# An H3 convolution and MLP stack: first block, first loads and first change of units rewritten

## The chip, the cores and the metric

The kernel runs on one core of a Trainium2 chip. A core has five engines with a queue each, worked in order: PE (TensorE, matmuls), DVE (VectorE), ACT (ScalarE), POOL (GpSimd) and SP (SyncE, which issues here all DMAs). The metric is the device time of one execution in microseconds; several executions are timed and their median is given. The profile of one execution gives the span of the program's instructions on the engines, and its own time.

## The reference

The input x is 2048 tokens by 1024 channels, fp32. Two layers follow each other twice, with the same weights both times:

```python
x = A_q
x = x + _A_ref(_layernorm(x, axis=-1), A_k, A_v, A_shift_k, A_ssm_k, A_ssm_D)
x = x + _B_ref(_layernorm(x, axis=-1), B_w1, B_b1, B_w2, B_b2)
x = x + _A_ref(_layernorm(x, axis=-1), A_k, A_v, A_shift_k, A_ssm_k, A_ssm_D)
x = x + _B_ref(_layernorm(x, axis=-1), B_w1, B_b1, B_w2, B_b2)
```

`_A_ref(q, k, v, ...)` shifts k by a four-tap causal filter, multiplies with v, convolves the product over the 2048 tokens with a long filter of each channel (through FFTs), adds `kv * ssm_D`, and multiplies with q. The convolution does not depend on x, so its result y serves both A layers; only the gate `layernorm(x) * y` is done twice. `_B_ref` is `relu(x @ w1 + b1)**2 @ w2 + b2` with 3584 hidden units.

## The kernel before

**Tiling.** Tokens are cut into 4 blocks of 512, and a block into 4 tiles of 128 tokens. A *unit* is one MLP layer on one block; ORDER gives the order of the units as (layer, block): (0,0), (1,0), (0,1), (0,2), (1,1), (0,3), (1,2), and the last entry does two blocks together. A unit runs over four chunks of 7 slices of 128 hidden units: steps of kind m1 (x times a piece of w1) and m2 (hidden times a piece of w2). A step is 12 or more matmuls of one weight piece of 128x512.

**Split numbers.** A matmul on fp32 is done as three on rounded numbers: each operand is a high part (a cast by ACT) and a low part (operand minus high part, a subtraction by DVE or POOL), lines 356, 357, 358. A weight piece is loaded by SP into `wr`, cast by ACT (line 1112) into the first half of `whl`, and its low part is made by DVE or POOL (line 1120; the letters in WLO choose). Some pieces are stored split (`wd_m`) and later loaded again as they are. `xh`, `xl` are the high and low part of the transposed, normalized input of a unit.

**The convolution** runs beside the MLP. A forward stream (`fwd_x`, `fwd_g`) brings k, v and the filter into another base: DMAs, ACT, DVE (lines 386 to 388 make the shifted product `fx`), PE transposes of it (line 441), PE matmuls (412, 475), DVE sums (504, 505), stores. A product stream multiplies (POOL, line 546, tile `cp`) and sums (DVE, line 550), goes back by PE (line 616), and stores y. After each MLP step the program runs some of each stream: `pace` gives how many products per step, FWD_RATE the forward steps. So the place of line 441's transposes in PE's queue is fixed when the program is written; PE waits there if DVE has not made `fx` yet.

**The first block** (`first_block`) does the convolution for block 0 without a stream: in a `Plan`, tasks with costs, dependencies and buffer rings are listed, and a search of 400 tries orders them by a list schedule. In it, for each of 8 groups c of 128 channels, x_part (lines 1227 to 1251) and g_part (1286 to 1293) are transforms on PE (line 1194) with a copy by ACT after each, `prods_both` multiplies them (1389 to 1403, DVE or POOL), `behind` goes back by PE, gates with the normalized q (1459) and adds to q (1468). `ln_part` takes the layernorm of q: bn_stats on DVE (1324), bn_aggr (1330), the reciprocal root by ACT Sqrt and six small DVE operations (1335 to 1344), and the scaling (1355 on DVE, 1358 on ACT). At its end the same is done for the gated sum (`tail_stats`, `tail_moments`, `tail`), with transposes (1498) and the splits into `xh`, `xl` (1505, 1507); the first weight pieces (`weight`, 1517, 1518) are loaded there too, and their matmuls are the first of unit 0. Filters need a patch: row 0 of the filter tile of a group is overwritten by a 1x128 DMA from the tile `first` (filter plus ssm_D). In the trace this is `xh<-xh`; `xh<-kT` is k, `fx<-vT` is v, `xh<-ssmT` the filter, `yh<-fwd` and `xh<-pro` the transform tables (all these live in the memory of `xh`, `yh`).

**The first change of units** goes from unit (0,0) to (1,0), on the same tokens, so the output of the last chunk is gated and normalized on the spot, for tiles 0 and 1 and then for 2 and 3 (`chain`), while PE does half steps of the other tiles (steps with fewer than 4 tiles). `evict1` adds the result to `accs` and takes bn_stats (1768, 1769), stage 0 and 1 make the scale (1735, 730 to 747, 1744), stage 2 gates (ACT 1750, DVE 1757, 1759) and takes bn_stats again (1763), stages 3 and 4 make the second scale, 5 and 6 normalize (1798, 1800), 7 and 8 transpose (1809), 9 and 10 split (1817, 1818). CHAIN gives for each stage after how many steps it is written.

Of the kernel before, what the change touches and what calls it, by code (L numbers as in the profile page):

```python
# [20 lines left out]
P = 128  # L21
# [31 lines left out]
PAD_C, PAD_P, PAD_M = 104, 56, 32  # L53
# [13 lines left out]
CHAIN = ((2, 3, 3, 7, 8, 8, 9, 13, 13, 14, 14), (2, 3, 3, 7, 8, 8, 9, 12, 12, 13, 13))  # L67
NORM = "VAVA"
# [181 lines left out]
def tile_h3_mlp(ctx: ExitStack, tc: tile.TileContext, q, kT, vT, shk, ssmT, ssmD, w1, b1, w2, b2,  # L250
# [54 lines left out]
    SY.dma_start(sgn, sgn_t)  # L305
    eph = const.tile([P, 2], F32)
    V.memset(eph[:, 0:1], EPS)
    V.memset(eph[:, 1:2], -0.5)
# [9 lines left out]
    SY.dma_start(b1t[:, 0:FT], b1)  # L318
# [838 lines left out]
    def first_block():  # L1157
# [24 lines left out]
        def dma(dst, src, r=(), w=(), cost=740, key=None):  # L1182
            pl.add([("D", cost)], lambda e: SY.dma_start(dst(), src()), r, w, lat=2000)

        with tc.tile_pool(name="pro", bufs=1) as pro:
# [19 lines left out]
            def kv_load(c):  # L1205
                k4 = sub("k4", 3, 0, [P, T + 3])
                v4 = new(cv, "fx", 4, [P, T])
                dma(lambda: k4.t, lambda: kT[c * P:(c + 1) * P, 0:T + 3], w=[k4])
                dma(lambda: v4.t, lambda: vT[c * P:(c + 1) * P, 0:T], w=[v4])
                return k4, v4  # L1210
# [13 lines left out]
            def x_part(c, k4, v4):  # L1224
# [14 lines left out]
                for r in range(2):  # L1239
# [7 lines left out]
                    pl.add([("PE", 1850)], mm, [xt, *tabs], [oi])  # L1247
# [10 lines left out]
            def g_load(c):  # L1258
                raw = sub("lg", 2, 1560, [P, T])
                for e in range(2):  # L1260
                    dma(lambda e=e: raw.t[:, e * BL:e * BL + BL].rearrange("p (b c) -> p b c", b=BT),
                        lambda e=e: g_rows(0, c)[:, e], w=[(raw, e)], cost=370)
                dma(lambda: raw.t[0:1, 0:P], lambda: first.t[c:c + 1, 0:P], [first], [(raw, 0)], cost=10)
# [63 lines left out]
            def moments(st, n):  # L1327
# [5 lines left out]
                ve, sd, r, nm = (new(pre, nm, m, [P, n]) for nm, m in (("ve", 3), ("sd", 3), ("rs", 4), ("nm", 3)))  # L1333
                t = new(pre, "rt", 2, [P, n])
                pl.add([("V", 140, 1)], lambda e: V.tensor_scalar(ve.t, mv.t[:, :, 1], EPS, None, op0=OP.add),
                       al, [ve], lat=130)
                pl.add([("A", 190)], lambda e: A.activation(sd.t, mv.t[:, :, 1], AF.Sqrt, bias=epst), al, [sd])
                pl.add([("V", 140, 1)], lambda e: V.reciprocal(r.t, sd.t), [sd], [r], lat=130)
                pl.add([("V", 140, 1)], lambda e: V.tensor_mul(t.t, r.t, r.t), [r], [t], lat=130)
                pl.add([("V", 140, 1)], lambda e: V.tensor_mul(t.t, t.t, ve.t), [ve], [t], lat=130)  # L1340
# [386 lines left out]
    def chain(accs, b, xh, xl, ready):  # L1727
# [4 lines left out]
        def agg(st):  # L1732
            mv = st["mv"] = pre.tile([P, 2, 2], F32, name="mv3", bufs=2)
            for n in range(2):
                V.bn_aggr(mv[:, n], st["st"][:, n])
# [629 lines left out]
```

## Time and profile before

| what | value |
|---|---|
| median of 3 runs | 2678.97 us (2678.12 to 2685.03) |
| the profiled execution | 2684.3 us |
| its span | 2682.5 us |
| PE busy | 2623.8 us (98%) |
| DVE busy | 1985.1 us (74%) |
| ACT busy | 1124.1 us (42%) |
| POOL busy | 1034.1 us (39%) |
| DMA moved | 763.16 MB, 284 GB/s over the span |
| mean granted TensorE clock | 0.994 |

A page lists the busy time of each engine, the chain of work that ended last, and the groups of instructions with their mean duration and the idle time before them. Here one engine is busy nearly all the time, so what is left to win or lose stands in its idle stretches, and in the stretches in which its clock was granted at half rate. They are found with the view of waits (who waited for whom), with the timeline (idle time before an instruction in brackets, with its releaser), and with windows (busy time and granted clock of a stretch).

### The profile page before, as it was taken

To read this page: it belongs to the slowest core of one execution; us is meant where nothing else is said; L and a number is where in the kernel's file an instruction comes from. 1 tells how busy PE (TensorE), PEld (TensorE's weight loads), DVE (VectorE), ACT (ScalarE), POOL (GpSimd) and SP (SyncE) were. 2 spreads that over 40 slices of the span, in tenths; PEclk is the share of its full clock that TensorE was granted. 3 is DMA by queue.
4 is the path that set the end of the run, shared out by engine and by line. 5 is a ranking of instruction groups with operands and counts; after the bars stand their busy time and mean duration, and the time that the engine had idled before them with its cause. 6 is when DMAs were issued, how large, how long until landed. Compare 5 with 4: busy or idle time off the path is not lost.

```text
span 2682.5 us, 36122 instructions
## 1 busy us (share of the span) xinstructions
PE 2623.8 (98%) x12388; PEld 2199.4 (82%) x12388; DVE 1985.1 (74%) x2881; ACT 1124.1 (42%) x1915; POOL 1034.1 (39%) x675
## 2 busy tenths in 40 slices
PE   7999899899999999999999999999999999999999
PEld 6888787787888888888888888888788778888887
DVE  7979788788887878779767775456778668777553
ACT  3444244343435323343233422345444585454342
POOL 2436665155551744417454275100100217536111
PEclk9999999999999999999999999999999999999999
DMA  7789988689989998888987888689889797878653
GB/s 247 255 306 310 296 291 283 240 282 357 348 296 315 313 331 307 275 292 308 337 307 261 297 292 314 201 273 312 299 298 307 263 340 255 263 249 316 232 193 121
DMA packets 380265, 763.16 MB, mean 284 GB/s; under 512 B 44064, under 2 KB 159408, under 8 KB 377008
## 3 DMA queue, kind: packets, MB, share of 16 engines
q1 hardware_dynamic: 380080, 760.85, 83.0%
q8 instruction: 98, 1.61, 0.2%
q14 instruction: 87, 0.71, 0.1%
HBM read 583.49 MB, written 177.21 MB: 284 GB/s over the span
## 4 chain that ended last, share of the span: by engine, by line
PE 79%; DMA 8%; DVE 5%; POOL 2%; issue 2%; ACT 2%; SPq 1%; DVEq 0%; POOLq 0%; ACTq 0%
PE p L357 23%; PE p L356 23%; PE p L358 23%; DMA whl<-wd_m 2%; PE pt L358 2%; PE pt L357 2%; PE pt L356 2%; PE p L1194 2%; DMA wr<-w 2%; DMA cg<-gd 1%; DVE whl L1120 1%; POOL cp L546 1%; DMA wd_m<-whl 0%; PE p L817 0%; DVE sm L550 0%
## 5 line engine op out<-in xcount | busy, mean ns | idle before, releaser
L546 POOL TENSOR_TENSOR cp<-cx,cg 128x384 f32<-128x384 f32 (+5 forms) x288 | 542.0, 1895 | 574.7 <-DVE sm L550 362.2
L356 PE MATMUL p<-xh,whl 128*128 128x512 f32 (+1 forms) x1504 | 578.4, 385 | 5.6 <-DMA whl<-wd_m 5.6
L358 PE MATMUL p<-xh,whl 128*128 128x512 f32 (+1 forms) x1504 | 574.1, 382 | 3.3 <-DVE whl L1120 2.8
L357 PE MATMUL p<-xl,whl 128*128 128x512 f32 (+1 forms) x1504 | 574.1, 382 | 0.1
L1112 ACT CAST whl<-wr 128x512 fp32r<-128x512 f32 x546 | 332.5, 619 | 468.4 <-PE p L358 278.6
L1120 DVE TENSOR_TENSOR whl<-wr,whl 128x512 fp32r<-128x512 f32 x486 | 421.0, 877 | 135.0 <-ACT whl L1112 130.2
L356 PE MATMUL p<-whl,rh 128*128 128x512 f32 x1204 | 475.4, 395 | 6.0 <-DMA whl<-wd_m 5.2
L357 PE MATMUL p<-whl,rh 128*128 128x512 f32 x1204 | 471.2, 391 | 2.8 <-POOL whl L1120 1.7
L358 PE MATMUL p<-whl,rl 128*128 128x512 f32 x1204 | 470.6, 391 | 0.0
L356 PEld LDWEIGHTS p<-xh,whl 128*128 128x128 f32 x1504 | 284.7, 189 | 60.8 <-issue 4.9
L358 PEld LDWEIGHTS p<-xh,whl 128*128 128x128 f32 x1504 | 284.2, 189 | 58.2 <-DVE whl L1120 3.0
L357 PEld LDWEIGHTS p<-xl,whl 128*128 128x128 f32 x1504 | 284.5, 189 | 52.4 <-DVE xl L1507 0.3
L1597 DVE TENSOR_TENSOR rl<-wr,rh 128x512 fp32r<-128x512 f32 x140 | 138.6, 990 | 182.5 <-ACT rh L1594 182.4
L1120 POOL TENSOR_TENSOR whl<-wr,whl 128x512 fp32r<-128x512 f32 x60 | 86.7, 1448 | 484.4 <-ACT whl L1112 438.1
L356 PEld LDWEIGHTS p<-whl,rh 128*128 128x128 f32 x1204 | 227.3, 189 | 54.1 <-issue 3.3
L357 PEld LDWEIGHTS p<-whl,rh 128*128 128x128 f32 x1204 | 227.1, 189 | 50.2 <-DVE whl L1120 2.7
L358 PEld LDWEIGHTS p<-whl,rl 128*128 128x128 f32 x1204 | 227.0, 189 | 47.5
L550 DVE TENSOR_REDUCE sm<-cp 128x128 f32<-128x384 f32 (+5 forms) x288 | 249.4, 874 | 12.3 <-POOL cp L546 12.3
L1589 ACT ACTIVATE wr<-p,b1t 128x512 f32<-128x512 f32 x138 | 95.2, 690 | 371.9 <-PE p L358 371.0
L1717 DVE TENSOR_TENSOR acc<-p,acc 128x512 f32<-128x512 f32 x152 | 99.7, 686 | 81.3 <-PE p L358 81.3
L696 POOL TENSOR_TENSOR sm<-sm 128x512 f32<-128x512 f32 x48 | 69.1, 1440 | 132.4 <-DVE sm L550 118.8
L358 PE MATMUL p<-whl,tq 128*128 128x512 f32 x276 | 107.4, 389 | 0.0
(384 smaller groups left out, 4282.3 us busy)
## 6 DMA issues: line engine op xcount, KB each, us to landing
whl<-wd_m SPq DMA_DIRECT2D x318, 512.0 KB, 5.6
wr<-w SPq DMA_DIRECT2D x442, 256.0 KB, 5.6
wd_m<-whl SPq DMA_DIRECT2D x70, 512.0 KB, 6.1
wr<-td SPq DMA_DIRECT2D x112, 256.0 KB, 5.1
cx<-xd SPq DMA_DIRECT2D x48, 512.0 KB, 5.7
cg<-gd SPq DMA_DIRECT2D x48, 512.0 KB, 7.0
tq<-hd SPq DMA_DIRECT2D x24, 1024.0 KB, 6.9
gd<-fg SPq DMA_DIRECT2D x72, 256.0 KB, 6.7
```

The source lines that it names most:

```text
L356: PE.matmul(o, lh, rh, start=start, stop=False)
L357: PE.matmul(o, lh, rl, start=False, stop=False)
L358: PE.matmul(o, ll, rh, start=False, stop=stop)
L546: G.tensor_mul(pr.rearrange("p c i -> p i c"), xt[:, 0:j + 1], gt[:, j::-1])
L550: V.tensor_reduce(sm[:, ty, jj], st["pr"], axis=AX.X, op=OP.add)
L696: E.tensor_add(s[:, 1:3], s[:, 1:3], s[:, 0:1].to_broadcast([P, 2, s.shape[2]]))
L1112: A.copy(t[:, 0], raws[n]["t"])
L1120: ENG[e[n % len(e)]].tensor_sub(t[:, 1], raws[n]["t"], t[:, 0].bitcast(F32))
L1194: PE.matmul(o, lh, r, start=start, stop=stop)
L1589: A.activation(r, st["o"], AF.Relu, bias=b1t[:, st["f"]:st["f"] + 1])
L1597: V.tensor_sub(st["lo"], st["r"]["t"], st["hi"].bitcast(F32))
L1717: V.tensor_add(accs[tt][:, d], o, accs[tt][:, d])
```

## The change

1. **Statistics of the first block on ACT.** `ln_part` no longer uses bn_stats: for each of the four tiles of q one ACT pass (Copy with scale -1/1024 and accum_out) sums the tile to minus its mean, and one (Square with that as bias) sums the squared differences. The reciprocal root is one `pow` with -0.5 on POOL, with two or three small POOL operations around it, here and in `moments`, which the tail keeps using after bn_stats. Scaling on DVE now is multiply and add with r and -mean*r.
2. **Ordered first loads, later weights.** HEAD ranks the first DMAs: k, the row for the patch, v, the filter, the tables. `sgn` and `b1` are loaded after them. The loads of the first eight weight pieces depend on a matmul of group 4 (W_AFTER, the key "late").
3. **The first change of units.** Tile 0 (or 2) of a half gets its sum from `scalar_tensor_tensor` with accum_out in the add itself (`summed`, 1742 after), and its squares from one ACT pass (`spread_a`, 1748 after); the other tile keeps bn_stats. Scales are made one tile at a time by three POOL operations (`scale_of`, 1758 to 1760 after). Gating is staged: tile 0 in stage 1, tile 1 in stage 2, with the normalization of tile 0 between them. CHAIN's numbers change, the splits of tile 2 and 3 come one or two steps earlier, NORM is "AAVA".
4. **Pace.** In half steps no products are run (rate 0 instead of a tenth), and PACE_SLACK for blocks 1 and 2 goes from 74 to 80, which spreads the same products over fewer steps. Weights are advanced before the streams in all half steps. PAD_P, a spacer in memory, goes from 56 to 120 columns.

Core of the diff:

```diff
@@
-PACE_SLACK = {1: 74, 3: 10}
+HEAD = {"k": 0, "f": 1, "v": 2, "g": 3, "t": 4, "p": 5, "d": 6}
+W_AFTER = 4
+PACE_SLACK = {1: 80, 3: 10}
-CHAIN = ((2, 3, 3, 7, 8, 8, 9, 13, 13, 14, 14), (2, 3, 3, 7, 8, 8, 9, 12, 12, 13, 13))
-NORM = "VAVA"
+CHAIN = ((2, 3, 5, 7, 8, 6, 9, 13, 13, 14, 14), (2, 3, 5, 7, 8, 6, 9, 11, 12, 12, 13))
+NORM = "AAVA"
@@ first_block
+            rank = 0 if head is None else HEAD[head] * 1e7 - 1e9
+            pl.add([("D", cost)], lambda e: SY.dma_start(dst(), src()), r, w, lat=2000, rank=rank)
@@ moments, ln_part
-                pl.add([("A", 190)], lambda e: A.activation(sd.t, mv.t[:, :, 1], AF.Sqrt, bias=epst), al, [sd])
-                pl.add([("V", 140, 1)], lambda e: V.reciprocal(r.t, sd.t), [sd], [r], lat=130)
...
+                pl.add([("G", 900)], lambda e: G.tensor_tensor(r.t, ve.t, eph[:, 1:1 + n], op=OP.pow), [ve], [r], lat=130)
+                pl.add([("G", 250)], lambda e: G.tensor_mul(nm.t, nm.t, r.t), [r], [nm], lat=130)
...
-                    for i in range(2):
-                        half_stats(st, k, x, i, keys[4 * i:4 * i + 4])
-                moments(st, len(ts))
+                    pl.add([("A", 1130)], lambda e, x=x, t=t, k=k: A.activation(
+                        ns[t].t, x.t, AF.Copy, scale=-1.0 / D, accum_out=nm.t[:, k:k + 1]), keys, [(nm, k), *spare])
+                    pl.add([("A", 1230)], lambda e, x=x, t=t, k=k: A.activation(
+                        ns[t].t, x.t, AF.Square, bias=nm.t[:, k:k + 1], accum_out=ss.t[:, k:k + 1]),
+                        [(nm, k), *keys], [(ss, k), *spare])
@@ chain
+        def summed(st, n, d, z):
+            x = accs[st["tts"][n]][:, d * 512:(d + 1) * 512]
+            V.scalar_tensor_tensor(x, z, 1.0, x, op0=OP.mult, op1=OP.add, accum_out=st["c"][:, 4 + d:5 + d])
+        def spread_a(st):
+            c = st["c"]
+            V.tensor_scalar(c[:, 0:1], c[:, 4:5], c[:, 5:6], -1.0 / (root * D), op0=OP.add, op1=OP.mult)
+            junk = ml.tile([P, D], BF16, name="yt", bufs=2)
+            A.activation(junk, accs[st["tts"][0]], AF.Square, scale=1.0 / root, bias=c[:, 0:1], accum_out=c[:, 1:2])
+            scale_of(st, 0, c[:, 1:2], c[:, 0:1], root)
+        def scale_of(st, n, var, m, k):
+            o = st["rn"][:, n]
+            G.tensor_add(var, var, epst)
+            G.tensor_tensor(o[:, 0:1], var, eph[:, 1:2], op=OP.pow)
+            G.tensor_scalar(o[:, 1:2], m, o[:, 0:1], k, op0=OP.mult, op1=OP.mult)
...
@@ the steps
-            rate *= 0.1
+            rate = 0.0
```

**What moves on SP, at the start.** Ahead of the change, SP's first loads in the first block:

```order
L1183 DMA xh<-ssmT 8x128
L1183 DMA xh<-kT 128x515
L1183 DMA xh<-ssmD 8x128
L1183 DMA xh<-pro 128x1024
L1183 DMA xh<-ssmT 128x2x128
L1183 DMA fx<-vT 128x512
L1183 DMA yh<-inv 128x256
L1183 DMA xh<-kT 128x515
L1183 DMA xh<-ssmT 128x2x128
L1183 DMA xh<-xh 1x16x8
L1183 DMA yh<-fwd 128x512
```

and with it:

```order
L1184 DMA xh<-kT 128x515
L1184 DMA xh<-ssmT 8x128
L1184 DMA xh<-ssmD 8x128
L1184 DMA fx<-vT 128x512
L1184 DMA xh<-ssmT 128x2x128 x2
L1184 DMA yh<-fwd 128x512
L1184 DMA xh<-pro 128x1024
L1184 DMA xh<-xh 1x16x8
```

The table `fwd` moved from behind the patch to ahead of it, k and v moved forward, and the second k and the table `inv` moved behind the patch.

**What moves on ACT, in the first block.** ACT's queue with the change, from the first copy of a g_part on (L1371 and L1373 are the passes for the statistics, L1238 the copy that x_part's matmuls read, L1357 the scaling):

```order
L1249 COPY sx<-p_218 128x2x4x64
L1373 ACTIVATE cp,sd<-cg,nm 128x1024
L1371 ACTIVATE cp,nm<-cg 128x1024
L1238 COPY fg<-p_261 128x512
L1371 ACTIVATE px,nm<-cx 128x1024
L1373 ACTIVATE cp,sd<-cg,nm 128x1024
L1289 ACTIVATE sg<-p_269 128x2x4x64
L1373 ACTIVATE px,sd<-cx,nm 128x1024
L1228 ACTIVATE p_309<-xh,shkt 128x512
L1373 ACTIVATE cp,sd<-cx,nm 128x1024
L1249 COPY sx<-p_291 128x2x4x64
```

The passes stand between the copies that PE's next matmuls read; before, only the copies and six casts of weights stood there.

**What moves on DVE, in the change of units.** The gating of tiles 2 and 3, ahead of the change (L1757 and L1759 gate, L1763 is bn_stats, L1120 the low part of a weight piece):

```order
L1757 TENSOR_TENSOR p_4978<-p_4978,px 128x512
L1757 TENSOR_TENSOR p_4980<-p_4980,px 128x512
L1759 TENSOR_TENSOR acc<-acc,p_4978 128x512
L1759 TENSOR_TENSOR acc<-acc,p_4980 128x512
L1763 BN_STATS st_4977<-acc 128x6 x2
L1757 TENSOR_TENSOR p_4986<-p_4986,px 128x512
L1757 TENSOR_TENSOR p_4988<-p_4988,px 128x512
L1759 TENSOR_TENSOR acc<-acc,p_4986 128x512
L1759 TENSOR_TENSOR acc<-acc,p_4988 128x512
L1763 BN_STATS st_4977<-acc 128x6 x2
L1120 TENSOR_TENSOR whl<-wr,whl 128x512
```

and with it (L1779 and L1742 gate tile 2, L1779 and L1782 tile 3, L1822 is bn_stats):

```order
L1779 TENSOR_TENSOR p_4878<-p_4878,px 128x512
L1779 TENSOR_TENSOR p_4880<-p_4880,px 128x512
L1742 SCALAR_TENSOR_TENSOR acc,nr<-p_4878,acc 128x512
L1742 SCALAR_TENSOR_TENSOR acc,nr<-p_4880,acc 128x512
L1746 TENSOR_SCALAR nr<-nr 128x1
L1120 TENSOR_TENSOR whl<-wr,whl 128x512
L1779 TENSOR_TENSOR p_4927<-p_4927,px 128x512
L1779 TENSOR_TENSOR p_4929<-p_4929,px 128x512
L1782 TENSOR_TENSOR acc<-acc,p_4927 128x512
L1782 TENSOR_TENSOR acc<-acc,p_4929 128x512
L1822 BN_STATS st_4882<-acc 128x6 x2
```

The weight's low part moved from behind twelve operations of both tiles to behind five of one.

More of the change, by code (lines that the diff above doesn't have):

```diff
@@ L304, in tile_h3_mlp @@
     sgn = const.tile([P, 2], F32)
-    SY.dma_start(sgn, sgn_t)
-    eph = const.tile([P, 2], F32)
+    eph = const.tile([P, NT + 1], F32)
     V.memset(eph[:, 0:1], EPS)
-    V.memset(eph[:, 1:2], -0.5)
+    V.memset(eph[:, 1:], -0.5)
     epst = eph[:, 0:1]
@@ L1515, in weight @@
                 hi, lo = (hl, 0), (hl, 1)
[L1516 removed]
+                dma(lambda: raw.t, lambda: w1[c * FC + f, :, 4 * kh:4 * kh + 4], r=["late"], w=[raw])
                 pl.add([("A", a_cost(512))], lambda e: A.copy(hl.t[:, 0], raw.t), [raw], [hi])
```

161 lines of the change are left out of this document (81 added, 80 removed).

## The prediction

> **What bounds the kernel now.** I read the page first, then the windows by stage, then the waits of PE, then the timeline around each wait.
>
> ```profile
> span 2682.5 us, 36122 instructions
> PE 2623.8 (98%) x12388; PEld 2199.4 (82%) x12388; DVE 1985.1 (74%) x2881; ACT 1124.1 (42%) x1915; POOL 1034.1 (39%) x675
> ```
>
> PE is idle for 2682.5 - 2623.8 = 58.7 us. No matmul leaves the program, so a change of this kind can only win idle time and time at a low clock.
>
> ```profile
> core 0: us, PE busy (x) PEld busy (x) DVE busy (x) ACT busy (x) POOL busy (x), PEclk, DMA share, GB/s
> 0.00:12.50 12.50, 1.10 (x4) 0.74 (x5) 3.48 (x10) 3.19 (x5) 0.69 (x6) 1.00 0.59 176
> 12.50:38.00 25.50, 25.44 (x132) 22.54 (x132) 18.46 (x30) 9.09 (x17) 2.65 (x2) 1.00 0.91 291
> 38.00:60.00 22.00, 18.16 (x98) 16.40 (x99) 20.45 (x29) 10.78 (x20) 8.22 (x7) 0.84 0.75 241
> 60.00:106.00 46.00, 45.79 (x280) 41.93 (x278) 44.09 (x60) 17.12 (x31) 28.01 (x22) 1.00 0.72 224
> 106.00:127.50 21.50, 16.82 (x138) 15.41 (x138) 19.25 (x52) 10.31 (x21) 5.75 (x7) 1.00 0.82 294
> 255.00:310.00 55.00, 45.88 (x206) 38.25 (x206) 47.70 (x68) 19.89 (x37) 32.23 (x27) 0.91 0.90 295
> 475.00:535.00 60.00, 52.09 (x306) 44.79 (x305) 45.07 (x97) 22.56 (x38) 12.77 (x11) 0.97 0.64 230
> 640.00:1900.00 1260.00, 1259.12 (x5882) 1054.08 (x5881) 924.71 (x1313) 470.73 (x826) 506.62 (x278) 1.00 0.86 301
> ```
>
> The idle time is in the start (11.4), the first block (up to 127.5, where unit 0's matmuls begin), unit 0 (255 to 310) and the first change of units (475 to 535). From 640 to 1900 PE is never idle for long: there is nothing to win there. In the first block DVE is nearly as full as PE (44.1 of 46 us), ACT is not.
>
> ```profile
> PE p L441 <- DVE fx L1233: 14.2, 3, 10.4
> PE p L356 <- DMA whl<-wd_m: 10.8, 9, 2.9
> PE pt L441 <- DVE fx L388: 9.8, 4, 7.3
> PE p L358 <- DVE whl L1120: 2.8, 1, 2.8
> PE pt L616 <- DVE fg L505: 2.4, 1, 2.4
> ```
>
> Those are the sums by releaser: DVE ends most of them. A stall has a second cost, the clock after it:
>
> ```profile
> 41.60:47.50 5.90, 5.82 (x21) 0.54 1.02 327
> 304.10:310.20 6.10, 6.05 (x18) 0.53 1.06 294
> 449.00:452.50 3.50, 3.41 (x14) 0.62 0.00 0
> 521.20:525.30 4.10, 4.02 (x21) 0.58 0.56 195
> ```
>
> These windows (PE alone; fourth figure the granted clock) follow the stalls of 3.68, 7.26, 2.35 and 2.79 us. Lost work is (1 - clock) x length: 2.7, 2.9, 1.3 and 1.7 us.
>
> **The start.** PE's first product waits for the table `fwd`, which SP issues behind the patch, which waits for the filter:
>
> ```profile
> 3.68 0.42 SPq L1183 DMA_DIRECT2D xh<-ssmT  x1
> 8.84 0.63 SPq L1183 DMA_DIRECT2D xh<-xh  x1
> 9.51 0.57 SPq L1183 DMA_DIRECT2D yh<-fwd  x1
> 9.52 0.69 DVE L1233 TENSOR_TENSOR fx<-p,fx 128x512 f32<-128x512 f32 x1 [1.03 <-DMA fx<-vT]
> 12.52 2.90 PE L1194 MATMUL p<-fg,yh 128*128 128x256 f32 x6 [1.07 <-DMA yh<-fwd]
> ```
>
> With the change k is issued second and v fifth, and `fwd` no longer waits. But PE's first product is now g_part, which needs the patch. The filter is issued sooner (about 3.2 instead of 3.7) with less ahead of it; by the 5.1 us it took here I put its landing at 7.3 and the patch's issue end at 7.9. The patch of this trace was issued at 8.84 to 9.47 and PE did not ask for it before 17.9; tiny loads issued at that time land in about 2.6 (it is 12.52 - 9.51 = 3.0 for the table). So PE starts at about 10.5: **-2.0** (bounds 0, if the filter lands as late as here, and -3.5).
>
> **The middle of the first block.**
>
> ```profile
> L1324 DVE BATCH_NORM_STATS2 st<-cg 128x6 f32<-128x512 f32 x4 | 2.6, 675 | 0.9 <-DMA cg<-q 0.9
> L1324 DVE BATCH_NORM_STATS2 st<-cx 128x6 f32<-128x512 f32 x4 | 2.5, 672 | 0.0
> 41.68 1.12 PE L441 MATMUL p<-ident,fx 128*128 128x128 f32 x4 [3.68 <-DVE fx L1233]
> L723 ACT ACTIVATE jk<-px,co x8: 1147/1150/1152, 2142.1 to 2191.5; 128x1024 bf16<-128x1024 f32 x8
> L723 ACT ACTIVATION_READ_ACCUMULATOR jk<-px,co x8: 185/186/188, 2143.2 to 2192.5; 128x1 f32 x8
> L725 POOL TENSOR_TENSOR co<-co,eph x8: 550/562/903, 2143.7 to 2193.4; 128x1 f32<-128x1 f32 x8
> ```
>
> DVE loses eight bn_stats, 2.6 + 2.5 = 5.1 us, just ahead of the operations whose lateness stops PE for 3.68 us at 41.68. ACT gains eight passes; line 723 is the same pass late in the program, 1.15 + 0.19, so 8 x 1.34 = 10.7 us. ACT is busy 9.1 of the 25.5 us from 12.5 to 38, so 19.8 fit, but its queue is in order, and the passes stand between the copies that PE reads (L1238 stands behind a pass on the tile of q that is loaded last). Walking the new queues with these durations I find two places where PE waits for ACT, about 1.0 and 1.3 us, and none as long as 3.68. I take 2.3 us of new stalls without a loss of clock: 2.3 - (3.68 + 2.7) = **-4.1**. Bounds: -6.4 (ACT hidden) and 0 (ACT takes over DVE's stall). The later weight loads free POOL and DMA early and cost nothing while their eight casts fit before the first weight matmul; ACT is busy 17.1 of 46 us there.
>
> **The end of the first block.** It is a chain over DVE, ACT and POOL, with PE waiting:
>
> ```profile
> 104.93 0.59 ACT L1248 COPY sx<-p 128x512 f32<-128x512 f32 x1 [1.14 <-PE p L1194]
> 109.69 0.69 DVE L696 TENSOR_TENSOR sm<-sm 128x512 f32<-128x512 f32 x1
> 118.68 0.27 DVE L1330 BATCH_NORM_AGGREGATE mv<-st 128x2 f32<-128x12 f32 x2
> 121.83 0.16 DVE L1344 SCALAR_TENSOR_TENSOR nm<-mv,rs 128x2 f32<-128x2 f32 x1
> ```
>
> The last transform on PE now comes after both pairs of return products instead of ahead of one (+0.9). From its copy to L696 there are 4.8 us here, with eight other DVE operations between; in the new order four, so about 3.3 (-1.4). From bn_aggr to the finished scale there are 3.0 us, six small DVE operations interleaved with four large ones; now four POOL operations, the pow at 0.56, the others shorter: about 1.9 (-1.1). Together **-1.6**, bounds +1 and -4.
>
> **Unit 0.** Nothing in its arithmetic changes, but its order does. The products start later (none in half steps) and are denser by 6 steps in some 230. So the transposes of line 441 come two to four steps later in PE's queue, at another distance from the evictions that fill DVE.
>
> ```profile
> 304.15 1.10 PE L441 MATMUL pt<-ident,fx 128*128 128x128 f32 x4 [7.26 <-DVE fx L388]
> ```
>
> The stalls here sum to 9.8 (L388) + 2.4 (L505), and 2.9 + 1.3 of clock, 16.4 us. The longest came when an eviction and the three shift operations stood close together on DVE; in the new order the next eviction is further ahead of them, and fewer products are done by the end of the unit. But DMA is at 0.90 there, and the backlog started with late loads, which stays. I take **-5**; bounds -16 (all gone) and +10 (one more like the longest, 7.26 + 2.9).
>
> **The change of units.**
>
> ```profile
> 521.28 0.43 PE L358 MATMUL p<-xh,whl 128*128 128x256 f32 x1 [2.79 <-DVE whl L1120]
> ```
>
> In 475 to 535 PE is idle 7.9 us. The longest, 2.79 + 1.7 of clock, waits for a low part that stands behind twelve gating operations on DVE; now it stands behind five, the bn_stats of one tile are gone (0.68 each by the rows above), and the small operations of the root are on POOL. I take 0.7 us for what is left: -3.8. Against it, POOL makes other low parts in this stage, and stands in order behind scales that wait for a 1.34 us pass on ACT; I take -1 for the other 5.1 us. **-4.8**, bounds -9 and +4.
>
> By the Trainium skill's "TensorE: Matmul & The Clock Gate", Part 1: The HAM clock gate, the clock halves after at least one idle window of about 3.4 us; here it halved after 2.35 and 2.79 too. By the page this term would be -3.1.
>
> The stalls on `whl<-wd_m` (10.8 us) lie mostly after the change of units, in an order that is nearly the same: 0, bounds ±4.
>
> **Sum**: -2.0 - 4.1 - 1.6 - 5 - 4.8 = -17.5. The profiled execution took 2684.3, 1.8 over its span and 5.3 over the median; so 2666.8 for it, and 2679.0 - 17.5 = **2661** for the median.
>
> **Rivals.**
> *Only the first block gains.* The stalls of unit 0 move without shrinking, and in the change of units POOL gives back what DVE gains: -7.7, so 2671. For it: both are matters of order, not of work. Against: DVE's load in the change does fall.
> *ACT becomes the bound of the first block.* The passes stand in order ahead of the copies PE reads, and stop it as long as DVE did: the middle gives 0, total -13.4, so 2666. For it: the q tiles land late (DVE waited 0.9 for one). Against: ACT's free 16 us.
> *All stalls named go.* -2 - 6.4 - 1.6 - 16.4 - 9 = -35, so 2644. For it: DVE ends nearly all of them. Against: the loads behind them stay.
> *Slower: more long stalls in unit 0.* One mechanism: the denser product stream makes DVE wait for POOL and POOL for `cx`, `cg` loads, and line 441's transposes, eight in this unit, meet the backlog. Each costs 7.26 + 2.9 = 10.2. Starting from -12.5 without the unit's -5, two more make +7.9 (2687); from the second on it is slower. For it: three of the four stalls on L388 are in this unit already, and DMA is at 0.9. Against: fewer products are due.
>
> **Chances**: forecast 0.52 (its own range 2653 to 2669), only the first block 0.20, ACT 0.10, all stalls 0.12, slower 0.06. About 0.3%, 8 us, is what a measurement of this kernel can tell from no change: the border is 2671. The forecast and "all stalls" are on the fast side, "only the first block" half, ACT mostly: 0.52 + 0.12 + 0.10 + 0.06 = 0.80, less 0.03 for what I have not seen: faster 0.77, same 0.17, slower 0.06. Range 2647 to 2674: it leaves out the slower case and half of the largest gain.
>
> **What would show it.** First product of PE at 10.5; no stall of over 2 us before 60, granted clock 1.0 in 38 to 60; first weight matmul at about 119.8 instead of 127.5; PE's waits for L388 at 5 us or less; no wait of over 2 us for L1120 in the change. It is wrong if PE waits for ACT's L1238 or L1289 for over 3 us in the first block, if waits of unit 0 sum to over 12 us, or if stalls after 640 appear.

## The result and the profile after

The change made the kernel slower: 2700.8 us median (2695.8 to 2705.2) against 2680.1 for the kernel before in the same comparison, a ratio of 1.0081 (95% interval 1.0068 to 1.0093). I had forecast 2661. The profiled execution of the changed kernel took 2695.8 us, the fastest of its four, that of before 2684.3, so this pair of profiles shows 11.5 of the 20.7 us.

The head of the page and the windows by stage of the changed kernel, in the columns of those shown of before (its first weight matmul is at 122 instead of 127):

```profile
span 2693.9 us, 36069 instructions
PE 2623.7 (97%) x12388; PEld 2195.2 (81%) x12388; DVE 1979.7 (73%) x2818; ACT 1137.9 (42%) x1937; POOL 1045.7 (39%) x707
```

```profile
core 0: us, PE busy (x) PEld busy (x) DVE busy (x) ACT busy (x) POOL busy (x), PEclk, DMA share, GB/s
0.00:12.50 12.50, 4.00 (x13) 3.26 (x14) 3.64 (x10) 2.76 (x4) 0.69 (x6) 1.00 0.70 188
12.50:38.00 25.50, 24.96 (x141) 22.37 (x140) 18.99 (x24) 21.12 (x38) 1.43 (x3) 1.00 0.89 287
38.00:60.00 22.00, 22.00 (x135) 20.32 (x134) 20.59 (x28) 8.15 (x15) 10.80 (x8) 1.00 0.84 261
60.00:106.00 46.00, 41.88 (x261) 38.12 (x261) 41.75 (x58) 18.35 (x33) 22.88 (x18) 1.00 0.77 251
255.00:310.00 55.00, 51.32 (x241) 42.94 (x239) 49.85 (x71) 19.81 (x37) 33.59 (x28) 1.00 0.98 328
475.00:535.00 60.00, 54.85 (x369) 49.59 (x368) 35.86 (x62) 33.04 (x54) 25.53 (x35) 1.00 0.64 222
600.00:660.00 60.00, 51.41 (x230) 41.85 (x230) 55.70 (x72) 24.93 (x43) 42.77 (x26) 0.94 0.98 346
640.00:1900.00 1260.00, 1250.28 (x5833) 1044.71 (x5832) 931.00 (x1305) 468.73 (x825) 513.77 (x282) 1.00 0.86 299
```

PE is busy for the same 2623.7 us as before (2623.8), and idle for 70.2 instead of 58.7: the 11.4 us by which this execution's span is longer are idle time of PE. The window that was full before, 640 to 1900, has lost 1259.12 - 1250.28 = 8.8 us of PE's work, and one that I had not looked at and that overlaps it, 600 to 660, is the worst behind the start. The same window of the kernel before:

```profile
600.00:660.00 60.00, 57.35 (x260) 47.52 (x259) 54.11 (x75) 22.94 (x42) 38.95 (x23) 0.97 0.99 351
```

The waits of PE, longest first (us in total, times, longest):

```profile
PE p L356 <- DMA whl<-wd_m: 12.3, 8, 3.6
PE p L441 <- DVE fx L1234: 8.2, 2, 7.8
PE pt L441 <- DVE fx L388: 8.2, 3, 3.8
PE p L357 <- DVE whl L1120: 4.7, 7, 1.7
PE p L358 <- DVE whl L1120: 4.1, 1, 4.1
PE p L357 <- POOL whl L1120: 2.9, 2, 2.2
```

The 14.2 us at the head of the list of before (L441 for fx of the first block, most of it the program's start) are down to 8.2, and L441 for L388 to 8.2 from 9.8. In their place stand waits for the low parts of weights (L1120). The longest of these is in the bad window; on PE and, ahead of it, on DVE's queue:

```profile
633.94 0.79 PE L358 MATMUL p<-xh,whl 128*128 128x512 f32 x1 [4.14 <-DVE whl L1120]
649.34 0.39 PE L357 MATMUL pt<-fx,fh 128*128 128x256 f32 x1 [1.56 <-DVE fx L402]
```

```profile
620.04 0.94 DVE L550 TENSOR_REDUCE sm<-cp 128x128 f32<-128x768 f32 x1
...
622.16 0.81 DVE L550 TENSOR_REDUCE sm<-cp 128x128 f32<-128x640 f32 x1
622.89 4.99 DVE L386 SCALAR_TENSOR_TENSOR fx<-fx,shkt 128x512 f32<-128x512 f32 x3
...
630.34 0.94 DVE L550 TENSOR_REDUCE sm<-cp 128x128 f32<-128x768 f32 x1
631.21 2.08 DVE L582 TENSOR_TENSOR yl<-sm,yh 128x256 fp32r<-128x256 f32 x2
633.21 0.68 DVE L1120 TENSOR_TENSOR whl<-wr,whl 128x512 fp32r<-128x512 f32 x1
```

DVE has no idle time in that stretch (no row has brackets), and the low part that PE needs stands behind a sum of products (L550), the low part of finished sums (L582) and a piece of the forward stream (L386). Some of these operations last longer here than elsewhere, while POOL multiplies products:

```profile
623.22 4.12 POOL L546 TENSOR_TENSOR cp<-cx,cg 128x640 f32<-128x640 f32 x2 [3.13 <-DMA cg<-gd]
...
631.36 1.65 POOL L546 TENSOR_TENSOR cp<-cx,cg 128x640 f32<-128x640 f32 x1 [4.02 <-DVE sm L550]
```

In this trace the low part of a weight piece on DVE (L1120) takes at most 0.70 us in the 338 cases in which no POOL operation runs beside it, and a median of 1.15, at most 2.91 us in the 186 cases in which one does; the sums of L550 over 768 columns take 0.94 us in both. By the same comparison L386 (at most 0.75 us alone) and L582 (0.42) are about 4.0 us longer between 622.9 and 633.2 than alone, as much as the stall of 4.14. So products weigh on DVE twice: by their sums, and while POOL multiplies. The total of this lengthening does not tell the kernels apart: from about 615 to 1400 all DVE operations together (each beyond the shortest tenth of its kind) are longer by 158 us here and 136 with the old pace, but 134 in the run with slack 76 (below), which is as slow as the change. What it costs is a matter of where it falls.

By stages that are cut at the same weight matmuls of the MLP in every kernel (the 1st, 1273rd, 1633rd, 1901st, 5001st and 6501st of the 8124 that write a tile `p`, in PE's order; the half steps of the change of units are the 1273rd to the 1632nd), with the same cuts for the runs of the next section, in us of the profiled executions:

| stage | before | changed | changed, old pace | before, new pace |
|---|---|---|---|---|
| first block | 127.0 | 122.3 | 121.8 | 124.5 |
| unit 0, up to the half steps | 334.2 | 331.6 | 331.2 | 337.2 |
| change of units | 90.6 | 88.1 | 88.5 | 91.7 |
| just behind it, to about 615 | 68.0 | 73.3 | 68.0 | 75.2 |
| to about 1400 | 775.7 | 787.4 | 775.3 | 790.3 |
| to about 1760 | 353.4 | 355.6 | 353.4 | 354.3 |
| the rest | 933.5 | 935.6 | 935.3 | 936.1 |

The first three stages gain 9.8 us; everything behind gives back 21.3. The last four rows are those that I had given nothing. The row to about 1400 holds the same 3660 matmuls in all four kernels; PE's idle time and lost clock ((1 - granted clock) x length) in it are together 4.9, 15.7, 2.9 and 19.8 us in the order of the columns. In the row ahead of it 348 matmuls stand with the new pace and 328 with the old one: there some 3 us are work that the pace moved.

### The profile page after: what moved, and what is told of

The parts are those of the page before. It is cut to its first block, busy times and chain, and to the rows that moved or that the text cites. A ratio compares the mean times of both kernels' runs of the same rounds, so it can differ in the third digit from the quotient of the medians.

```text
span 2693.9 us, 36069 instructions
## 1 busy us (share of the span) xinstructions
PE 2623.7 (97%) x12388; PEld 2195.2 (81%) x12388; DVE 1979.7 (73%) x2818; ACT 1137.9 (42%) x1937; POOL 1045.7 (39%) x707
## 4 chain that ended last, share of the span: by engine, by line
PE 70%; DMA 9%; DVE 8%; issue 3%; POOL 2%; ACT 2%; SPq 1%; DVEq 0%; ACTq 0%; POOLq 0%
PE p L357 21%; PE p L356 21%; PE p L358 21%; PE pt L358 2%; PE pt L357 2%; PE pt L356 2%; DMA whl<-wd_m 2%; DMA cg<-gd 2%; DMA wr<-w 1%; DVE whl L1120 1%; DMA wd_m<-whl 1%; POOL acc L1864 1%; DVE fx L386 1%; DVE sm L550 1%; DVE st L717 1%
## 5 line engine op out<-in xcount | busy, mean ns | idle before, releaser
L1120 DVE TENSOR_TENSOR whl<-wr,whl 128x512 fp32r<-128x512 f32 x486 | 422.0, 879 | 132.7 <-ACT whl L1112 125.5
L1607 DVE TENSOR_TENSOR rl<-wr,rh 128x512 fp32r<-128x512 f32 x140 | 149.7, 1070 | 175.2 <-ACT rh L1604 174.8
L550 DVE TENSOR_REDUCE sm<-cp 128x128 f32<-128x384 f32 (+5 forms) x288 | 249.6, 874 | 29.2 <-POOL cp L546 29.2
L1120 POOL TENSOR_TENSOR whl<-wr,whl 128x512 fp32r<-128x512 f32 x60 | 86.7, 1448 | 425.6 <-ACT whl L1112 204.3
```

What stands on the lines that cost most here:

```text
L550: V.tensor_reduce(sm[:, ty, jj], st["pr"], axis=AX.X, op=OP.add)
L1120: ENG[e[n % len(e)]].tensor_sub(t[:, 1], raws[n]["t"], t[:, 0].bitcast(F32))
L1607: V.tensor_sub(st["lo"], st["r"]["t"], st["hi"].bitcast(F32))
```

## The experiments

Three theories stood at first: the pace (part 4 of the change) moved products and the forward stream, the spacer moved buffers, or the new chain of the change of units was at fault.

**The old pace in the changed kernel.**

```diff
-PACE_SLACK = {1: 80, 3: 10}
+PACE_SLACK = {1: 74, 3: 10}
-            rate = 0.0
+            rate *= 0.1
```

> The changed kernel with the old pace (products at a tenth of the rate in half steps, slack 74); everything else new. Theory A (the pace makes the loss): products stand again as before, 10 instead of 0 in the half steps and 6 instead of 14 in the first 14 full steps behind them; so PE keeps its lead of 6 to 10 us over the kernel before at the 2250th weight matmul (the changed kernel has lost it there, +0.9), the stalls at 601 to 650 (8.6 us with their clock) shrink to about the 2.7 us of before, and the late ones (10 us from 880 on) go as well: time 2675 to 2685. Theory B (the spacer moves the buffers in memory, and loads and engines meet there): nothing changes before or behind the change of units, 2697 to 2705. Theory C (the new chain of the change of units is what collides with the loads): the lead is still lost between the 1750th and the 2250th matmul, 2693 to 2703.

Measured: 2675.3 us (2669.6 to 2677.8), a ratio of 0.9987 (0.9978 to 0.9997): 25 us less than the changed kernel, and the stalls of 600 to 660 are gone.

```profile
600.00:660.00 60.00, 59.58 (x280) 49.48 (x279) 58.58 (x72) 26.27 (x45) 39.59 (x24) 1.00 1.03 382
```

DVE is fuller here than in the changed kernel (58.6 of 60 us against 55.7), and so is DMA, yet PE waits for 0.4 us. So a full engine alone isn't what stops PE; it matters what stands in its queue ahead of what PE needs next.

**The new pace in the kernel before**, the same edit the other way round:

> The kernel before with only the new pace (rate 0 in half steps, slack 80). Theory A: the loss comes without the rest of the change: no lead of 4 to 5 us from the first block, and some 15 us lost behind the change of units, so 2690 to 2702. Theories B and C: the pace moves stalls about and costs nothing, 2673 to 2683.

Measured: 2708.0 us (2702.5 to 2711.2), ratio 1.0107 (1.0092 to 1.0122), slower by 30 us against 2678.1, more than the upper end expected. The pace alone makes the loss, and in the same stages (table above).

**The old spacer**, in the changed kernel and in the one with the old pace (`PAD_P` 56 instead of 120):

> The changed kernel with the spacer PAD_P back at 56 columns. Its order of instructions is that of the changed kernel. Theory B: the late stalls (0.95 at 882, 1.05 at 924, 2.05 at 1173, 1.72 at 1247, 1.6 at 1519, 3.62 at 1925) shrink and the durations of DVE's and POOL's operations fall by some per cent: 2680 to 2690. Theories A and C: 2695 to 2706, same stalls.

> The changed kernel with the old pace (2675.3) and the old spacer of 56 columns. If the spacer's place matters as the two runs of the changed kernel with either spacer suggest (2700.8 and 2707.3, unclear): 2678 to 2684. If not: 2672 to 2678.

Measured: 2707.3 us (2697.5 to 2711.4) with the new pace, and 2674.3 (2670.3 to 2678.5) with the old one. The first is no gain, the second differs by 1 us from the run with the wide spacer. The spacer is not the cause.

**Only the tenth of the rate put back; then three slacks.** Now the pace was to be taken apart:

```diff
-            rate = 0.0
+            rate *= 0.1
```

with `PACE_SLACK` at 80 as changed, and at 77 and 71.

> The changed kernel with only the tenth of the rate in half steps put back; the slack stays 80. Theory A, in the form that the rate in half steps decides and the slack does not: the products stand as with the old pace (6 in half steps, 5 in the first 14 full steps), so the time is that of the run with the whole old pace within 4 us, 2675 to 2688. If the slack decides: 2695 to 2703. Theories B and C: 2695 to 2705.

> The changed kernel with a tenth of the rate in half steps, and slack 77, between the 74 of the run with the old pace (2675.3) and the 80 of the run with the tenth alone (2692.8). Theory DENSITY (more products per step cost time as such, some 3 us per unit of slack): 2682 to 2687. Theory FIT (each value makes another order, and 74 is one that fits; its neighbours lose 5 to 20 us in no order): anything from 2678 to 2700, not in line.

> The same with slack 71, below the old value. Theory DENSITY: thinner products, 2665 to 2672. Theory FIT: slower than at 74 too, 2679 to 2700.

Measured: 2692.8 us (2690.5 to 2693.9) at 80, 2687.8 (2687.0 to 2690.3) at 77, 2675.3 at 74, 2687.1 (2680.9 to 2690.6) at 71. My form of the theory, that the slack does not matter, fell: from 74 to 80 costs 17.5 us. But it isn't density either, since fewer products per step (71) are 12 us slower than 74. 74 is a value to which this order fits, and the values tried on both sides, 71 and 77, miss it.

**No products in half steps, at slack 76.**

```diff
-PACE_SLACK = {1: 80, 3: 10}
+PACE_SLACK = {1: 76, 3: 10}
```

> The changed kernel with no products in half steps as it is, but slack 76 instead of 80. The products lie as in the changed kernel: none in half steps, 14 in the first 14 full steps behind the change. If the empty half steps make the loss (what is left undone there is run behind the change): 2694 to 2704, with the same stalls at 600 to 660. If the slack makes it: 2680 to 2690.

Measured: 2701.6 us (2699.6 to 2705.0). With empty half steps the slack changes nothing between 76 and 80 (2700.8): here the half steps decide. Slack 74 with empty half steps throughout was not run.

**Which half steps.** There are 8 at the start of unit 0 and 52 in the change of units. They are not alike, by a detail that I had read over. The loop that runs after each step is:

```python
        while todo > 0:
            x = next(pds, 0)
            ...
            elif x is None:
                fwd_tick()
                todo = 0
```

A product that finds its data missing pushes the forward stream one step. At the start of unit 0 no product has data, so a tenth of the rate, which is too little for a product, still gives the forward stream 8 steps; with rate 0 it gets none. In the program's order the first product then comes in step 33 instead of 29, and the debt of products (due by the pace, not run) is 3.1 instead of -0.2 when the change of units begins. It is frozen through the change and worked off behind it: 14 products in the first 14 full steps instead of 6. The two kinds of half steps apart, both with slack 74:

```diff
-            rate = 0.0
+            rate *= 0.1 if s < 16 else 0.0
```

> The changed kernel with slack 74, a tenth of the rate in the first 8 half steps of unit 0 and rate 0 in the 52 half steps of the change. The forward stream then starts as before, the products owe nothing at the change (-0.22 instead of 3.09), and 9 instead of 14 are run in the first 14 full steps behind it. Theory START (the loss comes from the 8 steps at the start): time within 5 us of the run with the old pace, 2671 to 2681, no stall over 2 us in 600 to 660. Theory CHANGE (the empty half steps of the change make the loss, whatever is owed): 2690 to 2702.

and the other way round (`rate *= 0.0 if s < 16 else 0.1`):

> The changed kernel with slack 74, rate 0 in the first 8 half steps of unit 0 and a tenth of the rate in the change. The products owe 2.1 at the change and 9 are run in its half steps, 3 in the first 14 full steps. Theory START: the forward stream is late as in the changed kernel, 2688 to 2702. Theory CHANGE: 2671 to 2681.

| rate in the 8 half steps at the start | rate in the 52 of the change | slack | us (range) | ratio |
|---|---|---|---|---|
| a tenth | a tenth | 74 | 2675.3 (2669.6 to 2677.8) | 0.9987 |
| a tenth | 0 | 74 | 2689.9 (2688.2 to 2691.3) | 1.0041 |
| 0 | a tenth | 74 | 2702.2 (2700.0 to 2706.9) | 1.0089 |
| 0 | 0 | 76 | 2701.6 (2699.6 to 2705.0) | 1.0087 |
| 0 | 0 | 80 (the change) | 2700.8 (2695.8 to 2705.2) | 1.0081 |

The 8 steps at the start alone cost 26.9 us, as much as the whole change. Rate 0 in the change costs 14.6 when the start is as before, and nothing visible on top of a late start. So neither theory holds as it was put. START expected the run with the start as before within 5 us of the old pace; CHANGE fits that run (2690 to 2702 expected), but expected 2671 to 2681 for the other. Either edit alone loses, and every other placing of the products that was tried loses 12 to 27 us.

The run with rate 0 at the start alone also shows what the loss does not need. It runs 3 products in the first 14 full steps behind the change, fewer than the 6 of the old pace, and still loses as much as any: its idle time and lost clock from about 615 to 1400 are 23.4 us, with waits for stored weight pieces (5.8 us) and for L582 (3.7) at the head. What it shares with the changed kernel is the late forward stream. How a stream that starts four steps late comes to cost this much there is not shown.

**What is late behind the change: DVE or the loads.** In the changed kernel's own order, 13 stores of split weights (6.8 MB) left out; then the sums of products cut short; then both:

```diff
+            if 158 <= now[0] < 200:
+                WD[key] = next(iter(WD.values()))
+                return
             WD[key] = dram.tile([P, 2, 512], F32, name="wd_" + "_".join(map(str, key)))
```

```diff
-            V.tensor_reduce(sm[:, ty, jj], st["pr"], axis=AX.X, op=OP.add)
+            pr = st["pr"][:, :, 0:1] if 158 <= now[0] < 420 else st["pr"]
+            V.tensor_reduce(sm[:, ty, jj], pr, axis=AX.X, op=OP.add)
```

> The changed kernel without the 13 stores of split weight pieces (512 KB each, 6.8 MB) that are written in the first 42 full steps behind the change of units; later loads of these pieces read another stored piece, so the output is not the reference's, and the order on PE, DVE, ACT and POOL is the same. Theory DMA (behind the change of units the DMA engines are full for some 100 us, and work that comes late there is paid on PE): 6.8 MB at 0.35 MB/us are 19 us of transfers less, so the stalls at 601 to 650 (8.6 us) shrink to under 3 us, PE's lead over the kernel before at the 2250th weight matmul is -7 to -11 instead of +0.9, and the time is 2686 to 2694. Rival ENGINES (fourteen products in fourteen steps load DVE and POOL, and the low parts of weights stand behind their sums): the stalls stay, 2697 to 2703.

> The changed kernel, with the sums of products (line 550) that are run from the change of units to about 1300 us cut to the first of their 4 to 10 addends: the output is not the reference's, the order on all engines is the same, and DVE has 0.5 to 0.9 us less to do per product, some 45 us in 600 to 1300 and 20 us in 550 to 660. Theory DVE (behind the change DVE's queue is full, the denser products put their sums ahead of the low parts of weights and of the conversions that PE waits for, lines 1120 and 402): the stalls at 630 to 650 (5.7 us, and 3.4 of clock) and at 1173 and 1247 (3.8) fall to under 3 us together, time 2684 to 2692. Rival PLACE (what is late there is not DVE's load but the distance in the queues between a conversion and its reader, which stays): the stalls shrink by less than half, 2694 to 2703.

> The changed kernel with both the short sums (2691.0 alone) and without the 13 stores (2703.1 alone); the output is not the reference's, the order on PE, DVE, ACT and POOL is the changed kernel's. If the stalls behind the change have two covers, DVE and the loads, either of which is enough, both together bring more than the 10 us of the sums: 2676 to 2685. If the loads have no part, 2688 to 2694.

Measured: 2703.1 us (2698.4 to 2705.5) without the stores, 2691.0 (2686.8 to 2698.6) with short sums, 2692.8 (2687.8 to 2696.9) with both. The window 600 to 660 without the stores, and then with short sums:

```profile
600.00:660.00 60.00, 51.75 (x224) 41.69 (x223) 51.56 (x66) 23.77 (x42) 39.67 (x23) 0.95 0.88 300
```

```profile
600.00:660.00 60.00, 55.67 (x256) 45.34 (x255) 53.62 (x79) 25.98 (x46) 45.97 (x27) 1.00 1.01 372
```

Without the stores the DMA share falls from 0.98 to 0.88, and PE waits as long as in the changed kernel (8.25 against 8.59 us): room for transfers is not what is lacking there. With the sums out of DVE's way the wait halves (4.33), and the granted clock is whole. The short sums bring 9.8 us, and 10.3 in the pair without the stores; from about 615 to 1400 idle time and lost clock fall from 15.7 to 6.8 us. Short sums with the old pace were not run, but there this stretch has only 2.9 us to win. DVE's other operations and POOL's products are still in place in these runs, and were not taken apart.

**More loads in the kernel with the old pace**, the opposite test:

```diff
+        if 158 <= s < 172:
+            for e in range(2):
+                SY.dma_start(extra[s % 2][:, e], w1[e, :, 0:4])
```

> The changed kernel with the old pace, and 28 idle transfers of 256 KB (7.3 MB, a weight piece copied to a place that nobody reads) issued in the first 14 full steps behind the change of units. Theory DMA: 7.3 MB at 0.35 MB/us are 21 us of transfers in a stretch that is full: the lead of 13.7 us at the 2250th weight matmul shrinks to between -4 and +6, time 2683 to 2695. Rival ENGINES: the loads have enough lead, 2674 to 2680.

Measured: 2688.8 us (2688.3 to 2690.5), 13.5 more than without, for 7.3 MB. Its long waits of PE between 570 and 660, summed by releaser, are others than those of the changed kernel:

```profile
PE p L356 <- DMA whl<-wd_m: 6.7, 5, 2.5
PE pt L356 <- ACT fx L417: 2.7, 1, 2.7
```

Here PE waits for stored weight pieces, not for low parts. So the stretch behind the change has no room for more DMA either; but that is not what the changed kernel lacks there.

**What the other parts of the change are worth**, with the old pace: the first block and its loads without the new change of units, and the new change of units alone in the kernel before.

```diff
-CHAIN = ((2, 3, 5, 7, 8, 6, 9, 13, 13, 14, 14), (2, 3, 5, 7, 8, 6, 9, 11, 12, 12, 13))
-NORM = "AAVA"
+CHAIN = ((2, 3, 3, 7, 8, 8, 9, 13, 13, 14, 14), (2, 3, 3, 7, 8, 8, 9, 12, 12, 13, 13))
+NORM = "VAVA"
...
```

> The changed kernel with the old pace and the old change of units: what is left is the first block with its loads (and the spacer). If the first block alone brings what the trace shows (weight matmuls begin 5 us earlier) and the new change of units brings the 4.8 us that I forecast, this run takes 2678 to 2682, 3 to 6 more than the run with the old pace (2675.3); if the new change of units brings nothing, 2673 to 2677.

> The kernel before with only the new change of units (its weights advanced ahead of the streams; old first block, old pace, old spacer). If the change of units is worth 4.8 us: 2672 to 2675. If it is worth nothing, 2676 to 2681. If it loses, over 2682, with waits of PE for low parts made by POOL.

Measured: 2676.8 us (2673.0 to 2683.3), ratio 0.9993 (0.9981 to 1.0004), with the first block alone; 2675.4 (2671.8 to 2677.4), ratio 0.9984 (0.9975 to 0.9993), with the change of units alone. The interval of the first one reaches past 1, so its 2 us are not shown, and the second lies between what was expected for a chain that brings 4.8 us and for one that brings nothing. Both together with the old spacer have the lowest median, 2674.3 us, ratio 0.9983 (0.9973 to 0.9992). So these parts gain 2 to 5 us together and do not add up.

In the change of units itself (the 1273rd to the 1632nd weight matmul) the new chain does gain. With the old pace it takes 85.3 to 88.5 us in five profiles, and the old chain takes 90.6 (the kernel before) and 93.3 (the first block alone). Part of that is lost again: from about 615 to 1400 the changed kernel with the old pace takes 775.3 against 771.3 with the first block alone; the new chain alone loses nothing there (772.7 against 775.7 before).

**The stall near 1916.** The longest wait there is 0.9 to 1.4 us in the kernels with the old pace, and 1.9 to 5.5 in all with another. The stream that transforms weights for the last units begins when the last product is done: in step 548 with the old pace, in 546 with the change. Only this beginning was moved:

```diff
-        if u >= WMAKE and len(done) == NB and not tgen:
+        if u >= WMAKE and len(done) == NB and s >= 548 and not tgen:
```

> The changed kernel, with the stream that transforms weights begun at step 548 as with the old pace, instead of 546; only DVE's and SP's order changes, from about 1290 us on. If the two steps make the stall near 1925 (3.62 us and 1.7 of clock), it falls to 1.1 to 1.7 us and the time by 3 to 5, to 2695 to 2698; if not, it stays at 3 to 5 us, 2699 to 2703.

> The changed kernel with the old pace (2675.3), with that stream begun three steps later, at 551 instead of 548. If the place of the beginning makes the stall, it rises from 1.1 to 3 or more and the time to 2678 to 2682; if not, 2673 to 2678.

The first matmul behind the long wait there: in the changed kernel; with its stream begun in step 548; with the old pace; and with the old pace and the stream begun in 551.

```profile
1929.00 0.50 PE L356 MATMUL p<-xh,whl 128*128 128x512 f32 x1 [3.62 <-DMA whl<-wd_m]
```

```profile
1926.50 0.50 PE L356 MATMUL p<-xh,whl 128*128 128x512 f32 x1 [1.40 <-DMA whl<-wd_m]
1931.38 0.47 PE L356 MATMUL p<-xh,whl 128*128 128x512 f32 x1 [1.86 <-DMA whl<-wd_m]
```

```profile
1905.86 0.50 PE L356 MATMUL p<-xh,whl 128*128 128x512 f32 x1 [1.10 <-DMA whl<-wd_m]
...
1915.59 0.47 PE L356 MATMUL p<-xh,whl 128*128 128x512 f32 x1 [0.60 <-DMA whl<-wd_m]
```

```profile
1911.04 0.79 PE L356 MATMUL p<-xh,whl 128*128 128x512 f32 x1 [5.03 <-DMA whl<-wd_m]
```

Measured: 2696.2 us (2695.4 to 2702.2), 4.5 less than the changed kernel, and 2677.7 (2673.3 to 2680.6), 2.4 more than the old pace alone; the ranges overlap in both cases. In the second run the stall grew as expected, and the last row of the table of stages is 939.2 instead of 935.3 us. In the first it did not fall to 1.1 to 1.7 us but came back in two parts, 1.40 + 1.86 instead of 3.62, and the last row is the same (935.3 against 935.6). So the place of this beginning can make such a stall; that it makes the one of the changed kernel, and costs 4.5 us there, is not shown.

## Why the prediction was wrong, point by point

**The step that failed** is the one that gave nothing to the time behind the change of units: "in an order that is nearly the same: 0, bounds ±4", and "from 640 to 1900 ... there is nothing to win there". I had seen that the products stand elsewhere in unit 0 (84 instead of 90 of DVE's sums L550 by its end, in the two traces) and used it as a relief ("fewer products are due"). What is not run there is run later. I never asked where: it lands in the stretch in which DVE is at 54.1 of 60 us and DMA at 0.99 already before. A stretch in which PE never waits has nothing to win and everything to lose; I had read it for the first only. The four rows behind the change, at 0 in my sum, came to +21.3 us in this pair of profiles, and the runs put 25 us on the pace. The sign of being wrong that I named, "stalls after 640 appear", is what came. That products pile up right behind the change is only part of it, since the run with 3 products there and a late forward stream loses as much.

Of the 25.5 us, 9.8 go when the sums of products on DVE are cut short. The other 16 are not settled. Four profiles of the changed order (with either spacer, without the stores, and with the later weight stream) say where the loss lies, against three of the old pace with the same chain (with either spacer, and with the stream at 551): 1.7 us in the change of units, 4.4 just behind it (some 3 of them moved work), 14.8 from there to 1400 (the sums' part included). But no run takes those other waits away by their cause.

**Rivals.** The slower one had the right kind of mechanism (a stream's place in the queues meets a backlog) with 0.06, but in unit 0 and with more long waits on L388. There are three of 2.1 to 3.8 us now instead of one of 7.3 and one of 1.9, and their sum fell, 8.2 us instead of 9.8. "Only the first block gains" had POOL give back what DVE gains in the change of units; that came in part (below). The range of 2647 to 2674 left out all that happened.

**The start**, -2.0. The first product on PE is at 9.60 instead of 12.52 (forecast 10.5); it waits for the patch, as said, and the patch is issued at 6.51, when the filter has landed:

```profile
6.51 0.64 SPq L1184 DMA_DIRECT2D xh<-xh  x1
7.77 1.10 PE L441 MATMUL p<-ident,fx 128*128 128x128 f32 x4 [7.77 <-DVE fx L1234]
9.60 2.07 PE L1195 MATMUL p<-xh,yh 128*128 128x256 f32 x4 [0.73 <-DMA xh<-xh]
...
18.26 1.03 PE L1195 MATMUL p<-xh,yh 128*128 128x256 f32 x4
```

My landing of the filter at 7.3 did not follow from what I added up (3.2 + 5.1 would be 8.3, and what less ahead of it saves I did not work out); the filter was faster than either, and the path was right. But the first products run at half speed, 2.07 us for four against 1.03 later, as they did before (2.90 for six). In the changed kernel this lasts until about 14.7, before until 16.3 (matmuls of this size start every 0.43 us until then, and every 0.22 us after), so PE starts 2.9 us earlier and runs at full speed only 1.6 us earlier in this pair.

**The middle**, -4.1. No stall is over 0.5 us between 12.5 and 60 and the clock is whole in 38 to 60, as forecast; ACT's passes came to what was worked out (21.1 us of its 25.5 busy, forecast 19.8), and in this execution no wait for ACT's L1238 shows before 72. The 401st product starts at 86.8, against 92.8 before.

**The end**, -1.6: the wrong sign. From the 401st product to the first weight matmul it is 35.5 us, against 34.3 in the kernel before and in both other runs of its first block. The waits there:

```profile
103.24 2.02 PE L1195 MATMUL p<-sx,yh 128*128 128x128 f32 x16 [1.80 <-DVE sg L1292]
112.19 1.16 PE L1195 MATMUL p<-sg,yh 128*128 128x128 f32 x8 [1.57 <-ACT fg L1318]
117.58 1.10 PE L1506 MATMUL p<-ident,cp 128*128 128x128 f32 x8 [1.59 <-ACT cp L1357]
121.93 0.63 PE L1506 MATMUL p<-ident,cp 128*128 128x128 f32 x4 [1.05 <-DVE xl L1515]
```

I had shortened DVE's part of the chain and not asked who would be last instead; now ACT (L1318, L1357) ends 3.2 of these 6.0 us.

**The first block as a whole**: -7.7 forecast, -4.7 between the two profiles (127.04 to 122.32). But the old first block was profiled three times, with its first weight matmul at 127.04, 124.53 and 124.06, and the new one 17 times, 120.95 to 125.0, mean 122.7. So the mean gain is 2.5 us. The execution from which I took the stalls of 3.68 us and their clock was 5.3 us above the median, and I said so, but took its stalls at their full size: in the other two, 2.51 + 1.65 and 1.28 + 1.64 stand in that place, and no half clock.

**Unit 0**, -5: -2.6 in this pair of profiles (up to the half steps), the marker (waits for L388 at 5 us or less) missed with 8.2. Here one execution says little: of six profiles whose order is the same up to this point, four took 331 to 332 us and two 338.

**The change of units**, -4.8: -2.5 in this pair (90.6 to 88.1). With the same pace and first block on both sides the new chain brings more: 5.3 us in the kernel before (90.6 to 85.3), and 4.8 or more with the new first block (93.3 to between 85.3 and 88.5). So this term was about right in mechanism and size, as far as these profiles show. The wait of 2.79 us for L1120 on DVE is gone; a wait of 2.23 us for a low part that POOL makes has come, so the marker of no wait over 2 us was missed and POOL took back a part of what DVE gave.

## What to carry to other kernels

A stretch without idle time on the bounding engine is the place to look at when work is moved: ask of each deferred piece which stretch it lands in, and what stands in that queue ahead of the operand that is needed next. A rate that looks like a throttle of one stream may drive another; follow the loop that spends it, also where nothing is due. And stalls read from one execution are samples: where the profiled run lies above the median, its long stalls are part of the reason, and a gain counted from them should be cut accordingly.

## What the runs showed of the hardware

I had charged four stalls, of 2.35 to 7.26 us, with the half clock that stood behind them. The stretches after four stalls of the changed kernel (PE alone; the fourth figure is the granted clock), after 2.43, 2.25, 3.80 and 1.82 us of idle time in this order:

```profile
453.10:456.50 3.40, 3.40 (x19) 1.00 0.03 9
233.70:237.10 3.40, 3.39 (x17) 1.00 0.96 384
310.10:313.50 3.40, 3.38 (x13) 0.73 1.06 390
2194.70:2198.10 3.40, 3.35 (x14) 0.67 0.94 286
```

The stall of 1.82 us was followed by a half clock, those of 2.43 and 2.25 were not: the length alone does not decide. The Trainium skill's "TensorE: Matmul & The Clock Gate", Part 1: The HAM clock gate, says that the window in which activity is judged is free-running and does not reset when a kernel starts. If a stall does not reset it either, which no run here shows, the same stall may cost 1.7 us of clock, as behind the 2.79 us of the kernel before, or nothing; the four rows fit that.

The same order also differed by up to 7 us in unit 0 from run to run (330.8 to 338.2), so differences of a few us between two single profiles carry no weight in this kernel.
